# Spectral mixing and a maxout layer in one kernel: all stores on one queue, in more and smaller blocks

## The chip, the cores and the metric

The kernel runs on one core of one Trainium2 chip. The metric is device time in microseconds (us) from launch to end. Three runs of the kernel before took 436.36, 440.05 and 441.28 us, a median of 440.05 us. One more execution was profiled; all durations below come from that one.

A core has five engines that run their own instruction streams: TensorE (PE, matmuls; PEld is its weight load), VectorE (DVE), ScalarE (ACT), GpSimd (POOL) and SyncE (SP), which only starts transfers. SP and ACT start transfers on hardware queues, POOL on a software queue. 16 DMA engines move the data.

## What is computed

```python
def _attn_ref(x):                       # x: 8 x 3072 x 256
    X = np.fft.fft(x, axis=1)
    X = np.fft.fft(X, axis=2)
    return X.real.astype(np.float32)

def _moe_ref(x, w1, w2, w3, w_out):     # 24576 x 256, w: 256 x 768, w_out: 768 x 256
    h = np.maximum(np.maximum(x @ w1, x @ w2), x @ w3)
    return (h @ w_out).astype(np.float32)

def reference(**kwargs):
    ...
    x = attn_out.reshape(B * S, D)
    return _moe_ref(x=x, **moe_kwargs)
```

Each of 8 batches has 3072 tokens of 256 values. A two-dimensional Fourier transform is taken and its real part goes through three linear maps, a maximum over them, and an output map.

## The kernel before

**Mixing.** The transform over the sequence is split in two factors, and the transform over the 256 features is folded into the weights (`g_all`, `gd_all`, `gw`). For batch b the class `Mix` has these steps. `s` multiplies the loaded `xt` by a small table (through PSUM into `tb`). `y` writes `tb` to a DRAM buffer `db`, and `z` reads it back transposed into `yb` (four transfers, two for each value of `hh`); both are issued by SP, and z waits until y has landed. `x0` fills one column of `yb`. `k` makes the token tables `tE` (even part) and `tO` (odd part) from `yb`, in three column groups; after each odd group SP writes one row of `tO` to DRAM (`vd`), and `v` broadcasts it from there over 128 partitions (`vb`).

**Symmetry.** Token n and token 3072 - n have the same even part and opposite odd parts. So one pass over 1536 columns gives both: rows "plus" (n) and "minus" (the mirror rows).

**Units.** The main loop has 18 units per batch: 3 blocks of 512 columns by 6 chunks of 128 hidden values, 144 units in all. `begin` multiplies for the plus rows and writes `hp`; `finish` adds the difference `gd_all` x `tO` onto the same PSUM tiles (L489) and writes `hm`. In a plain unit this takes six matmuls of 512 columns, two ScalarE activations and two VectorE maxima. In a split unit (`is_split`) the third product is made ahead by `third` (L824), two units early: two matmuls, one ScalarE copy (`odd`), one VectorE sum with `vb` (`even`, L833), and two GpSimd sums `plus` and `minus` (L837). Then `begin` needs two matmuls, `finish` one, and each a VectorE operation (L846, L858). Odd units from 7 on are split, and even units 0, 4 and 8 of each batch but the first. `prev` holds the unit whose `finish` is still to come. If it is split, `finish` comes before the next `begin`; otherwise after it.

**Output.** When a block's six units are done, its output matmuls (`l2_block`, L553 and L576) are put in a queue and ten are taken in each following unit (`l2_some`). So a block's results are complete at the end of the sixth unit after it: block 2 of the batch before in unit 5, block 0 in unit 11, block 1 in unit 17. They stand in one of three buffers (`obufs`: `obuf` and the two halves of `kq`) as 128 partitions by 8 slots of 256 values: slots 0 to 3 plus rows, 4 to 7 minus rows.

**Order of the rows.** The columns of the tables, and so the partitions of the output buffers, are numbered by `ramp`. A slot has 96 partitions of one residue modulo 32 and 32 partitions of another. Each group is cut into two halves in opposite order, so that both the plus rows (ascending) and the minus rows (descending within each half) can be described by a regular pattern.

**Stores before.** `stores_plus` gives four transfers per block (48, 16, 48 and 16 partitions), for block 2 six, with one of 47 and one of 48 single rows. SP issues them as soon as the block is complete. `stores_minus` gives two per block (three for block 2), each over both halves in one pattern (`back`, with a leading count of 2). They are put in `waiting`, and GpSimd issues them in the next unit (`scatter`).

**What else is on the queues.** GpSimd issues the x loads (L115), in units 9 or 10 and 11 of a batch and 0 and 1 of the next. SP issues y (units 2 and 3), z0 and z1 (units 6 and 7), `vd` and `v` (units 12 to 16), each at its place in the program, and SP works strictly in this order.

**The last block.** `l2_last` takes the sub-blocks in the order 1, 2, 3, 0. Minus rows are computed there in flipped order (`flipped`, from reversed copies of `tE` and `tO`, and `hm` written reversed), and its stores go to ACT, SP and POOL in turn: twelve after sub-block 3 and eight at the end.

The table `ahead` (L802) says in which unit a mixing step for the next batch is emitted.

Of the kernel before, what the change touches and what calls it, by code (L numbers as in the profile page):

```python
# [20 lines left out]
def _reduce(nc, w, v, q, period):  # L21

    nc.vector.tensor_scalar(out=q, in0=v, scalar1=1.0 / period, scalar2=ROUND,
                            op0=ALU.mult, op1=ALU.add)
    nc.vector.tensor_scalar(out=q, in0=q, scalar1=-ROUND, scalar2=-period,
                            op0=ALU.add, op1=ALU.mult)
    nc.vector.tensor_tensor(out=w, in0=v, in1=q, op=ALU.add)


def _parts(g):  # L30
# [10 lines left out]
def kernel(  # L41
# [9 lines left out]
    nc = tc.nc  # L51

    B, S, D = x.shape
# [83 lines left out]
    def iota(t, pattern, base=0, cm=0):  # L137
        nc.gpsimd.iota(t, pattern, base=base, channel_multiplier=cm,
                       allow_small_or_imprecise_dtypes=True)
# [17 lines left out]
    def ramp(g):  # L157
        kv = kvec[:, 512 * g:512 * g + 512].rearrange("p (s c) -> p s c", s=4)
        n = 4 if g < 2 else 3
        iota(kv[:, 0:n, 0:96].rearrange("p s (a j) -> p s a j", a=2),  # L160
             [[1, n], [-1536, 2], [32, 48]], base=4 * g + 1 + 1536)
        iota(kv[:, :, 96:128].rearrange("p s (a j) -> p s a j", a=2),
             [[1, 4], [-512, 2], [32, 16]], base=12 + 1024 * g + 512)
        if g == 2:
            iota(kv[:, 3, 0:96].rearrange("p (a j) -> p a j", a=2), [[-768, 2], [16, 48]],
                 base=784)
            iota(kvec[:, NHALF:NHALF + 1], [[0, 1]], base=0)

    dvec = gen.tile([128, 128], FP32, tag="dvec")
# [339 lines left out]
    def rows_of(b):  # L509

        mine = out[b * S:(b + 1) * S, :]
        return mine, mine.rearrange("(j r) d -> j r d", r=32)

    def back(v):
        return v.rearrange("(a j) r d -> a j r d", a=2)[:, ::-1]

    def stores_plus(b, blk, buf, s0=0, s1=4):

        mine, v = rows_of(b)
        n = s1 if blk < 2 else min(s1, 3)  # L520
        for a in range(2):
            j = 48 - 48 * a
            yield v[j:j + 48, 4 * blk + 1 + s0:4 * blk + 1 + n, :], buf[48 * a:48 * a + 48, s0:n, :]
            j = 32 * blk + 16 - 16 * a
            yield v[j:j + 16, 12 + s0:12 + s1, :], buf[96 + 16 * a:112 + 16 * a, s0:s1, :]
        if n < s1:
            yield mine[784:784 + 46 * 16 + 1:16, :], buf[0:47, 3, :]
            yield mine[16:16 + 47 * 16 + 1:16, :], buf[48:96, 3, :]

    def stores_minus(b, blk, buf):  # L530

        mine, v = rows_of(b)
        n = 4 if blk < 2 else 3
        r = 32 - 4 * blk
        yield back(v[0:96, r - n:r, :]), buf[0:96, 8 - n:8, :]
        yield back(v[64 - 32 * blk:96 - 32 * blk, 17:21, :]), buf[96:128, 4:8, :]
        if n < 4:
            yield back(mine[NHALF:S - 15:16, :].unsqueeze(1)), buf[0:96, 4:5, :]

    def stores_turned(b, buf, s0, s1):  # L540

        mine, v = rows_of(b)
        n = min(s1, 3)
        for a in range(2):
            j = 48 - 48 * a
            yield v[j:j + 48, 24 - n:24 - s0, :], buf[80 - j:128 - j, 8 - n:8 - s0, :]
            yield v[16 - 16 * a:32 - 16 * a, 21 - s1:21 - s0, :], buf[16 * a:16 * a + 16, 8 - s1:8 - s0, :]
            if n < s1:
                yield mine[S - 768 - 768 * a:S - 15 - 768 * a:16, :], buf[80 - j:128 - j, 4, :]

    def l2_hidden(po, hcols):
        for jc in range(NJC):
# [4 lines left out]
    def l2_block(b, blk, hp, hm, te, to):  # L557

        buf = obufs.pop(0)
        obufs.append(buf)  # L560
        for sub in range(4):
            slot = blk * 4 + sub
            cp = slice(slot * 128, slot * 128 + 128)
            sp = slice(sub * 128, sub * 128 + 128)
            if sub % 2 == 0:
                pl = ps_f.tile([128, 512], FP32, name="pl", tag="ps")
                for i in range(2):
                    ci = (slot + i) * 128
                    nc.tensor.matmul(pl[:, i * 256:(i + 1) * 256], te[:, ci:ci + 128],
                                     gw[:, 0:256], start=True, stop=True)  # L570
                    yield
                even = even_pool.tile([128, 512], FP32, name="even", tag="even")
                nc.scalar.copy(out=even, in_=pl)
            lin = even[:, (sub % 2) * 256:(sub % 2 + 1) * 256]
            po = ps_o.tile([128, 512], FP32, name="po", tag="po")
            nc.tensor.matmul(po, to[:, cp], gw[:, 256:768], start=True, stop=True)  # L576
            yield
            yield
            yield from l2_hidden(po[:, 0:256], lambda jc: hp[:, jc, sp])
            yield from l2_hidden(po[:, 256:512], lambda jc: hm[:, jc, sp])  # L580
            nc.vector.tensor_tensor(  # L581
                out=buf[:, sub:8 - sub:7 - 2 * sub, :], in0=po.rearrange("p (h c) -> p h c", h=2),
                in1=lin.unsqueeze(1).to_broadcast([128, 2, 256]), op=ALU.add)
        for (dst, src) in stores_plus(b, blk, buf):
            store(nc.sync, dst, src)
        waiting.extend(stores_minus(b, blk, buf))

    def l2_last(hp, hm, te, to, flipped):

        buf = obufs.pop(0)  # L590
        ter, tor = flipped
        for sub in (1, 2, 3, 0):
            slot = 8 + sub
            cp = slice(slot * 128, slot * 128 + 128)
            sp = slice(sub * 128, sub * 128 + 128)
            sm = slice((3 - sub) * 128, (4 - sub) * 128)
            for (h, tev, tov, wo, hid) in (
                    (0, te[:, cp], to[:, cp], gw[:, 256:512], lambda jc: hp[:, jc, sp]),
                    (1, ter[:, sm], tor[:, sm], gw[:, 512:768], lambda jc: hm[:, jc, sm])):
                if h == 0 or sub == 0:  # L600
                    po = ps_o.tile([128, 512], FP32, name="po", tag="po")
                ph = po[:, h * 256:(h + 1) * 256]
                nc.tensor.matmul(ph, tev, gw[:, 0:256], start=True, stop=False)
                yield
                nc.tensor.matmul(ph, tov, wo, start=False, stop=True)
                yield
                yield from l2_hidden(ph, hid)
                stores = []
                if sub == 0:
                    nc.vector.tensor_copy(out=buf[:, 7 * h, :], in_=ph)  # L610
                    stores = (stores_turned(B - 1, buf, 0, 1) if h else
                              stores_plus(B - 1, 2, buf, 0, 1))
                elif h:
                    nc.vector.tensor_copy(out=buf[:, sub:8 - sub:7 - 2 * sub, :],  # L614
                                          in_=po.rearrange("p (h c) -> p h c", h=2))
                    if sub == 3:
                        stores = [*stores_plus(B - 1, 2, buf, 1, 4),
                                  *stores_turned(B - 1, buf, 1, 4)]
                for k, (dst, src) in enumerate(stores):
                    store((nc.scalar, nc.sync, nc.gpsimd)[k % 3], dst, src)  # L620

    def l2_mid():

# [23 lines left out]
        store(nc.sync, out[0: S * (B - 1) + 1: S, :], ot[0:B, 0:256])  # L647

    l2_queue = []
    waiting = []  # L650

    def scatter():

        while waiting:
            store(nc.gpsimd, *waiting.pop(0))

    def l2_some(n):
        while n > 0 and l2_queue:
            try:
# [131 lines left out]
    for b in range(2, B):  # L791
# [3 lines left out]
        for ch in range(8):  # L795
# [4 lines left out]
              7: ("z0", "z1"), 12: ("x",), 13: ("kO0",), 14: ("v0", "kE0", "kO1"),  # L800
              15: ("v1", "kE1"), 16: ("kO2",), 17: ("v2", "kE2", "end")}
    ahead = {1: ("s0", "s1"), 2: ("s2", "y0", "s3", "s6"), 3: ("s4", "s5", "y1", "u"),  # L802
             6: ("z0",), 7: ("z1",), 11: ("x",), 12: ("kO0",), 13: ("v0", "kE0", "kO1"),
             14: ("v1", "kE1"), 15: ("kO2",), 16: ("v2", "kE2", "end")}
    for b in range(B - 1):
        for u, whats in (ahead0, ahead)[min(b, 1)].items():
# [4 lines left out]

    def is_split(g):
        if g % 2 == 0:
            return UNITS <= g < B * UNITS and g % UNITS in (0, 4, 8)
        return 7 <= g < B * UNITS

    def operands(g):
# [46 lines left out]
    for g in range(B * UNITS):  # L864
# [4 lines left out]
        if jc == 0:  # L869
            hp = h_pool.tile([128, NJC, TOKB], BF16, name="hp", tag="hp")  # L870
            hm = h_pool.tile([128, NJC, TOKB], BF16, name="hm", tag="hm")
            if last:
                flipped = []
                for t, name in ((mm.tE, "tEr"), (mm.tO, "tOr")):
                    fl = h_pool.tile([128, TOKB], BF16, name=name, tag=name)
                    flipped.append(fl)
                    nc.gpsimd.tensor_copy(fl, t[:, 3 * TOKB - 1: 2 * TOKB - 1: -1])
        if prev is not None and is_split(prev[0]):
            finish(*prev)
            prev = None  # L880
        pses = begin(g, hp[:, jc, :])
        if prev is not None:
            finish(*prev)
        prev = (g, pses, hm[:, jc, ::-1] if last else hm[:, jc, :])
        for lead in (1, 2):
            if is_split(g + lead) and (lead == 1) == (g + lead == 7):
                third(g + lead)
        scatter()
        l2_some(10)
        if b == B - 1 and u in (1, 3):  # L890
            if u == 1:
# [8 lines left out]
            l2_queue.append(l2_last(hp, hm, mm.tE, mm.tO, flipped) if last else  # L900
                            l2_block(b, blk, hp, hm, mm.tE, mm.tO))

    scatter()
    l2_some(1000)

# [28 lines left out]
```

## Time and profile before

| | |
|---|---|
| median of three runs | 440.05 us |
| the profiled execution's own time | 433.8 us |
| its span, first to last instruction | 432.0 us |
| mean granted TensorE clock | 0.975 |
| PE busy | 383.7 us, 89% of the span |
| VectorE / GpSimd / ScalarE busy | 330.4 / 308.2 / 248.6 us |
| hardware queue q1 (SP) | 26.58 MB, 23.6% of 16 engines' span |
| software queue q0 (POOL) | 26.67 MB, 34.8% of 16 engines' span |
| store issues on POOL | 59, of them 43 from `kq` with 28.4 us busy |
| POOL stores, issue to landing | 8.1 to 15.8 us, median 11.7 |

The busy share in 40 slices shows when an engine works; PEclk is the granted TensorE clock in tenths.

```profile
PE   7799997998979979999979969999499999999990
PEclk9999999999999989999999989999799999999996
DMA  8999563867538582687747582575413644322343
```

The chain of work that ended last, by engine, shows 57% PE and 21% DMA:

```profile
PE 57%; DMA 21%; DVE 8%; issue 4%; ACT 3%; POOL 2%; SPq 2%; DVEq 0%; POOLq 0%; ACTq 0%
```

How to read the rest: in lists of waits, "A <- B: 13.5, 4, 5.5" says that A's engine stood idle for 13.5 us in 4 cases, 5.5 at most, until B had ended. In timelines the first number is the start from the span's begin, the second the duration in us; "SPq" is SP's own stream, and a DMA line there is the issue, not the transfer. TensorE matmuls are pipelined, and the profile's PE durations overlap: 512 columns take 0.22 us one behind the other.

### The profile page before, as it was taken

What the parts mean: (1) busy time and instruction counts of PE and PEld (TensorE: products, weight loads), DVE (VectorE), ACT (ScalarE), POOL (GpSimd) and SP (SyncE); (2) the same over time, 40 slices, a digit from 0 to 9 for tenths busy, and PEclk for the clock granted to TensorE, in tenths of its full rate; (3) what the DMA queues carried; (4) which work ended last, traced back from release to release, by engine and by line L of the source; (5) the groups of instructions that cost most, each with busy time, mean ns of one, the idle gap of its engine ahead of it and who ended that gap; (6) DMA issues with size and microseconds to landing.
All of it is one profiled execution on the core that took longest, in us unless ns stands there. A gap on an engine that the chain in (4) does not pass through costs nothing.

```text
span 432.0 us, 8171 instructions
## 1 busy us (share of the span) xinstructions
PE 383.7 (89%) x2769; PEld 238.6 (55%) x2818; DVE 330.4 (76%) x551; ACT 248.6 (58%) x454; POOL 308.2 (71%) x336
## 2 busy tenths in 40 slices
PE   7799997998979979999979969999499999999990
PEld 2455664565645546565645636565265666665670
DVE  7887976886688857798778847789277997898860
ACT  6887794666736756575836746576365537433400
POOL 9981676987487946988677955977358776879741
PEclk9999999999999989999999989999799999999996
DMA  8999563867538582687747582575413644322343
GB/s 126 162 179 182 132 138 92 137 145 171 123 82 164 158 170 71 121 168 161 147 96 152 140 180 86 104 143 133 130 46 83 147 122 113 86 66 60 89 110 106
DMA packets 72244, 54.24 MB, mean 126 GB/s; under 512 B 46717, under 2 KB 64900, under 8 KB 71347
## 3 DMA queue, kind: packets, MB, share of 16 engines
q0 software_dynamic: 39680, 26.67, 34.8%
q1 hardware_dynamic: 32106, 26.58, 23.6%
q10 hardware_dynamic: 416, 0.48, 0.4%
q8 instruction: 22, 0.36, 0.3%
q14 instruction: 20, 0.16, 0.1%
HBM read 36.95 MB, written 30.81 MB: 157 GB/s over the span
## 4 chain that ended last, share of the span: by engine, by line
PE 57%; DMA 21%; DVE 8%; issue 4%; ACT 3%; POOL 2%; SPq 2%; DVEq 0%; POOLq 0%; ACTq 0%
PE po L553 19%; DMA yb<-db 12%; PE pse L489 9%; DMA vb<-vd 4%; PE e L828 4%; PE pse L482 4%; PE d L830 3%; PE pse L483 3%; DMA vd<-tO 3%; PE pse L844 3%; PE po L576 3%; PE pse L845 3%; PE ps L393 2%; DVE hp L846 2%; DVE hm L858 2%
## 5 line engine op out<-in xcount | busy, mean ns | idle before, releaser
L837 POOL TENSOR_TENSOR plus<-even,odd 128x512 bf16<-128x512 f32 x90 | 114.4, 1271 | 105.6 <-DVE even L833 96.1
L837 POOL TENSOR_TENSOR minus<-even,odd 128x512 bf16<-128x512 f32 x90 | 114.1, 1268 | 0.0
L832 ACT ACTIVATE odd<-d 128x512 f32<-128x512 f32 x90 | 53.8, 598 | 66.7 <-PE d L830 57.7
L553 PE MATMUL po<-wout_bf,hp 128*128 128x256 bf16 x576 | 86.3, 273 | 0.0
L846 DVE SCALAR_TENSOR_TENSOR hp<-pse,plus 128x512 bf16<-128x512 f32 x90 | 61.7, 686 | 24.5 <-PE pse L845 11.4
L553 PE MATMUL po<-wout_bf,hm 128*128 128x256 bf16 x576 | 80.3, 277 | 0.0
L495 ACT ACTIVATE stmp<-pse 128x512 bf16<-128x512 f32 x108 | 64.6, 601 | 26.4 <-PE pse L483 11.3
L489 PE MATMUL pse<-tO,gd_all 128*128 128x512 bf16 x197 | 67.9, 387 | 11.1 <-DVE hp L846 9.1
L833 DVE SCALAR_TENSOR_TENSOR even<-vb,wcol,e 128x512 f32<-128x512 bf16 x90 | 66.4, 738 | 7.9 <-DMA vb<-vd 7.9
L553 PEld LDWEIGHTS <-hp 128*128 128x128 bf16 x576 | 56.5, 98 | 26.4 <-issue 0.3
L858 DVE SCALAR_TENSOR_TENSOR hm<-pse,minus 128x512 bf16<-128x512 f32 x90 | 61.7, 685 | 11.8 <-PE pse L489 10.2
L553 PEld LDWEIGHTS <-hm 128*128 128x128 bf16 x576 | 57.2, 99 | 18.2 <-issue 2.1
L496 DVE TENSOR_TENSOR hp<-pse,stmp 128x512 bf16<-128x512 f32 x54 | 37.2, 689 | 26.7 <-ACT stmp L495 22.5
L496 DVE TENSOR_TENSOR hm<-pse,stmp 128x512 bf16<-128x512 f32 x54 | 37.2, 690 | 10.2 <-ACT stmp L495 8.1
L581 DVE TENSOR_TENSOR kq<-po,even 128x512 f32<-128x512 f32 x60 | 41.0, 684 | 0.1
L122 ACT COPY xt<-xt 64x762 bf16<-64x762 bf16 (+1 forms) x48 | 39.7, 838 | 1.0
L483 PE MATMUL pse<-tO,g_all 128*128 128x512 bf16 x101 | 38.3, 379 | 0.5 <-issue 0.2
L482 PE MATMUL pse<-tE,g_all 128*128 128x512 bf16 x100 | 37.9, 379 | 0.7 <-DVE tE L460 0.4
L828 PE MATMUL e<-tE,g_all 128*128 128x512 bf16 x89 | 34.5, 387 | 3.2 <-DVE even L833 2.9
L576 PE MATMUL po<-gw,tO 128*128 128x512 bf16 x92 | 35.1, 382 | 0.0
L830 PE MATMUL d<-tO,gd_all 128*128 128x512 bf16 x90 | 34.9, 387 | 0.2
L499 POOL DMA_DIRECT2D out_dram<-kq x43 | 28.4, 666 | 5.8 <-DVE kq L614 3.6
(167 smaller groups left out, 500.4 us busy)
## 6 DMA issues: line engine op xcount, KB each, us to landing
xt<-in_x_dram POOLq DMA_DIRECT2D x14, 384.0 KB, 9.7
db<-tb SPq DMA_DIRECT2D x21, 192.0 KB
out_dram<-obuf SPq DMA_DIRECT2D x16, 192.0 KB
out_dram<-obuf POOLq DMA_DIRECT2D x8, 384.0 KB, 12.8
out_dram<-kq SPq DMA_DIRECT2D x16, 192.0 KB
out_dram<-kq POOLq DMA_DIRECT2D x8, 384.0 KB, 11.1
vb<-vd SPq DMA_DIRECT2D x23, 128.0 KB
xt<-in_x_dram POOLq DMA_DIRECT2D x7, 400.0 KB, 8.4
```

The source lines that it names most:

```text
L482: nc.tensor.matmul(pse[:, 0:n], g_all[:, jc, 2 * i, :], te, start=True, stop=False)
L483: nc.tensor.matmul(pse[:, 0:n], g_all[:, jc, 2 * i + 1, :], to, start=False, stop=True)
L489: nc.tensor.matmul(pse, gd_all[:, jc, i, :], to, start=False, stop=True, skip_group_check=True)
L495: nc.scalar.activation(out=stmp[:, 0:n], in_=pses[0][:, 0:n], func=AX.Relu)
L496: nc.vector.tensor_tensor(out=dst, in0=src3, in1=stmp[:, 0:n], op=ALU.max)
L553: nc.tensor.matmul(po, hcols(jc), wout_bf[:, jc * 256:(jc + 1) * 256], start=False, stop=(jc == NJC - 1), skip_group_check=True)
L828: nc.tensor.matmul(e3, g_all[:, jc, 2, :], te, start=True, stop=True)
L832: nc.scalar.activation(out=odd3, in_=d3, func=AX.Copy, scale=-0.5)
L833: nc.vector.scalar_tensor_tensor(out=even3, in0=vb, scalar=wcol[:, jc:jc + 1], in1=e3, op0=ALU.mult, op1=ALU.add)
L837: nc.gpsimd.tensor_tensor(out=dst, in0=even3, in1=odd3, op=op)
L846: nc.vector.scalar_tensor_tensor(out=dst, in0=pse2, scalar=0.0, in1=sums[g][0], op0=ALU.max, op1=ALU.max)
L858: nc.vector.scalar_tensor_tensor(out=dst, in0=pses[0], scalar=0.0, in1=sums.pop(g)[1], op0=ALU.max, op1=ALU.max)
```

## The change

- The order of rows is cut differently: the 96 partitions into 6 blocks of 16 (`MAIN`), the 32 into 4 blocks of 8 (`LOW`), and the extra slot of block 2 into 5 blocks of 19 and one single row (`LATE`). `ramp` and all store patterns follow.
- `stores_plus` gives one transfer per block of rows: 10 per block of columns, and 16 for block 2. `stores_minus` still gives one per group, over all its blocks at once (leading count 6, 4 or 5).
- SP issues plus and minus rows one after the other when the block is complete; `waiting` and `scatter` go.
- In the last block the plus rows are now the flipped ones (`hp` written reversed, `stores_turned` over plus slots), the minus rows are natural, and its 7 + 4 stores go to ACT and SP in turn.
- z0 and z1 of the next batch are emitted in unit 5, ahead of that unit's stores in SP's order.
- Unit 10 of each batch but the first is split as well.
- If both the waiting unit and the new one are split, `begin` of the new one now comes before `finish` of the waiting one.

```diff
+MAIN = (6, 16)
+LOW = (4, 8)
+LATE = (5, 19)
...
-    def back(v):
-        return v.rearrange("(a j) r d -> a j r d", a=2)[:, ::-1]
-
-    def stores_plus(b, blk, buf, s0=0, s1=4):
+    def back(v, n):
+        return v.rearrange("(a j) r d -> a j r d", a=n)[:, ::-1]
+
+    def stores_plus(b, blk, buf):
+
+        mine, v = rows_of(b)
+        n = 4 if blk < 2 else 3
+        for at, j0, (na, nj), r, m in ((0, 0, MAIN, 4 * blk + 1, n), (96, 32 * blk, LOW, 12, 4)):
+            for a in range(na):
+                j = j0 + nj * (na - 1 - a)
+                yield v[j:j + nj, r:r + m, :], buf[at + a * nj:at + a * nj + nj, 0:m, :]
+        if n < 4:
+            for a in range(5):
+                m = 1 + 19 * (4 - a)
+                yield mine[16 * m:16 * (m + 18) + 1:16, :], buf[19 * a:19 * a + 19, 3, :]
+            yield mine[NHALF:NHALF + 1, :], buf[95:96, 3, :]
+
+    def stores_minus(b, blk, buf, s0=0, s1=4):
...
+        r = 32 - 4 * blk
+        yield back(v[0:96, r - n:r - s0, :], MAIN[0]), buf[0:96, 8 - n:8 - s0, :]
+        yield (back(v[64 - 32 * blk:96 - 32 * blk, 21 - s1:21 - s0, :], LOW[0]),
+               buf[96:128, 8 - s1:8 - s0, :])
         if n < s1:
...
+            yield (back(mine[NHALF + 16:S - 15:16, :].unsqueeze(1), LATE[0]), buf[0:95, 4:5, :])
...
         for (dst, src) in stores_plus(b, blk, buf):
             store(nc.sync, dst, src)
-        waiting.extend(stores_minus(b, blk, buf))
+        for (dst, src) in stores_minus(b, blk, buf):
+            store(nc.sync, dst, src)
...
-                    store((nc.scalar, nc.sync, nc.gpsimd)[k % 3], dst, src)
+                    store((nc.scalar, nc.sync)[k % 2], dst, src)
...
-             6: ("z0",), 7: ("z1",), 11: ("x",), 12: ("kO0",), 13: ("v0", "kE0", "kO1"),
+             5: ("z0", "z1"), 11: ("x",), 12: ("kO0",), 13: ("v0", "kE0", "kO1"),
...
-            return UNITS <= g < B * UNITS and g % UNITS in (0, 4, 8)
+            return UNITS <= g < B * UNITS and g % UNITS in (0, 4, 8, 10)
...
-        if prev is not None and is_split(prev[0]):
+        if prev is not None and is_split(prev[0]) and not is_split(g):
             finish(*prev)
             prev = None
-        pses = begin(g, hp[:, jc, :])
+        pses = begin(g, hp[:, jc, ::-1] if last else hp[:, jc, :])
         if prev is not None:
             finish(*prev)
-        prev = (g, pses, hm[:, jc, ::-1] if last else hm[:, jc, :])
+        prev = (g, pses, hm[:, jc, :])
...
-        scatter()
```

More of the change, by code (lines that the diff above doesn't have):

```diff
@@ L159, in ramp @@
         n = 4 if g < 2 else 3
[L160 to L163, printed above, removed]
+        (a, j), (la, lj), (ea, ej) = MAIN, LOW, LATE
+        iota(kv[:, 0:n, 0:96].rearrange("p s (a j) -> p s a j", a=a),
+             [[1, n], [-32 * j, a], [32, j]], base=4 * g + 1 + 32 * (96 - j))
+        iota(kv[:, :, 96:128].rearrange("p s (a j) -> p s a j", a=la),
+             [[1, 4], [-32 * lj, la], [32, lj]], base=12 + 1024 * g + 32 * (32 - lj))
         if g == 2:
-            iota(kv[:, 3, 0:96].rearrange("p (a j) -> p a j", a=2), [[-768, 2], [16, 48]],
-                 base=784)
+            iota(kv[:, 3, 0:95].rearrange("p (a j) -> p a j", a=ea), [[-16 * ej, ea], [16, ej]],
+                 base=16 * (96 - ej))
+            iota(kv[:, 3, 95:96], [[0, 1]], base=NHALF)
             iota(kvec[:, NHALF:NHALF + 1], [[0, 1]], base=0)
@@ L512, in rows_of @@
         return mine, mine.rearrange("(j r) d -> j r d", r=32)
-    def back(v):
-        return v.rearrange("(a j) r d -> a j r d", a=2)[:, ::-1]
-    def stores_plus(b, blk, buf, s0=0, s1=4):
+    def back(v, n):
[13 more added lines that the diff above has]
+    def stores_minus(b, blk, buf, s0=0, s1=4):
         mine, v = rows_of(b)
         n = s1 if blk < 2 else min(s1, 3)
[L521 to L525, printed above, removed]
-        if n < s1:
[L527 to L538, printed above, removed]
+        r = 32 - 4 * blk
+        yield back(v[0:96, r - n:r - s0, :], MAIN[0]), buf[0:96, 8 - n:8 - s0, :]
+        yield (back(v[64 - 32 * blk:96 - 32 * blk, 21 - s1:21 - s0, :], LOW[0]),
+               buf[96:128, 8 - s1:8 - s0, :])
+        if n < s1:
+            yield (back(mine[NHALF + 16:S - 15:16, :].unsqueeze(1), LATE[0]), buf[0:95, 4:5, :])
     def stores_turned(b, buf, s0, s1):
@@ L543, in stores_turned @@
         n = min(s1, 3)
[L544 to L549, printed above, removed]
+        yield back(v[0:96, 9 + s0:9 + n, :], MAIN[0]), buf[32:128, s0:n, :]
+        yield back(v[64:96, 12 + s0:12 + s1, :], LOW[0]), buf[0:32, s0:s1, :]
+        if n < s1:
+            yield back(mine[16:NHALF - 15:16, :].unsqueeze(1), LATE[0]), buf[33:128, 3:4, :]
+            yield mine[NHALF:NHALF + 1, :], buf[32:33, 3, :]
     def l2_hidden(po, hcols):
@@ L597, in l2_last @@
             for (h, tev, tov, wo, hid) in (
-                    (0, te[:, cp], to[:, cp], gw[:, 256:512], lambda jc: hp[:, jc, sp]),
-                    (1, ter[:, sm], tor[:, sm], gw[:, 512:768], lambda jc: hm[:, jc, sm])):
+                    (0, ter[:, sm], tor[:, sm], gw[:, 256:512], lambda jc: hp[:, jc, sm]),
+                    (1, te[:, cp], to[:, cp], gw[:, 512:768], lambda jc: hm[:, jc, sp])):
                 if h == 0 or sub == 0:
@@ L610, in l2_last @@
                     nc.vector.tensor_copy(out=buf[:, 7 * h, :], in_=ph)
-                    stores = (stores_turned(B - 1, buf, 0, 1) if h else
-                              stores_plus(B - 1, 2, buf, 0, 1))
+                    stores = (stores_minus(B - 1, 2, buf, 0, 1) if h else
+                              stores_turned(B - 1, buf, 0, 1))
                 elif h:
@@ L616, in l2_last @@
                     if sub == 3:
-                        stores = [*stores_plus(B - 1, 2, buf, 1, 4),
-                                  *stores_turned(B - 1, buf, 1, 4)]
+                        stores = [*stores_turned(B - 1, buf, 1, 4),
+                                  *stores_minus(B - 1, 2, buf, 1, 4)]
                 for k, (dst, src) in enumerate(stores):
-                    store((nc.scalar, nc.sync, nc.gpsimd)[k % 3], dst, src)
+                    store((nc.scalar, nc.sync)[k % 2], dst, src)
     def l2_mid():
@@ L649 @@
     l2_queue = []
[L650 to L655, printed above, removed]
     def l2_some(n):
@@ L901 @@
                             l2_block(b, blk, hp, hm, mm.tE, mm.tO))
-    scatter()
     l2_some(1000)
```

## The prediction

> **What bounds the kernel now.** I read the page's chain of waits first, then the waits of the engines, then a table with one stretch for each batch, then SyncE's own timeline. Everything is made against the profiled execution: its span is 432.0 us, its own time 433.8 us, so 1.8 us lie around the span; the median of the three runs, 440.05 us, is 6.25 us above it. I work out a difference on the profile and add it to the median.
>
> The waits name two transfers:
>
> ```profile
> PE ps L458 <- ACT yb L448: 13.5, 4, 5.5
> PE pse L489 <- DVE hp L846: 9.1, 15, 1.2
> PE e L828 <- DVE even L833: 2.9, 2, 1.5
> ...
> ACT yb L447 <- DMA yb<-db: 20.7, 5, 7.0
> ...
> DVE even L833 <- DMA vb<-vd: 7.9, 3, 3.0
> ```
>
> Columns: total us, times, longest. TensorE waits for ScalarE's `yb`, and ScalarE waits for the gather `yb<-db` (the z step). Second comes the `vb` broadcast, without which VectorE cannot start the third sums of the next batch.
>
> The stretches run from the first `hp` write of a batch to that of the next, batches 1 to 6:
>
> ```profile
> 73.61:123.73 50.12, 44.81 (x325) 27.95 (x331) 38.40 (x61) 30.71 (x55) 37.30 (x38) 1.00 0.64 136
> 123.73:174.09 50.36, 45.51 (x324) 28.34 (x330) 38.79 (x62) 30.65 (x55) 37.38 (x38) 0.97 0.63 135
> 174.09:222.28 48.19, 44.99 (x329) 28.12 (x333) 38.46 (x62) 30.80 (x56) 37.28 (x38) 1.00 0.66 141
> 222.28:273.32 51.04, 45.59 (x324) 28.30 (x330) 38.70 (x61) 30.72 (x55) 37.38 (x38) 0.97 0.60 133
> 273.32:327.15 53.83, 46.65 (x328) 28.86 (x332) 38.88 (x62) 30.82 (x56) 36.17 (x36) 0.94 0.48 112
> 327.15:372.61 45.46, 44.26 (x328) 27.98 (x332) 38.58 (x61) 24.20 (x47) 34.89 (x34) 1.00 0.46 114
> ```
>
> After each stretch stand its length, then PE, PEld, DVE, ACT and POOL busy, then the granted clock. Batch 6 has neither wait: 45.46 us with TensorE busy for 44.26. That is the floor. The five before it lie 4.66, 4.90, 2.73, 5.58 and 8.37 above it, together 26.2 us. Part of this is clock: it is 0.51 for 3.5 us right after the PE waits of 2.9 and 3.5 us, and for 6.9 us after the one of 5.5.
>
> SyncE in batch 1:
>
> ```profile
> 85.78 3.11 SPq L415 DMA_DIRECT2D db<-tb  x1
> 88.99 4.87 SPq L499 DMA_DIRECT2D out_dram<-kq  x6
> 93.95 4.42 SPq L421 DMA_DIRECT2D yb<-db  x4
> 102.85 3.51 SPq L499 DMA_DIRECT2D out_dram<-obuf  x4
> 108.31 0.23 SPq L463 DMA_DIRECT2D vd<-tO  x1
> 113.28 0.34 SPq L467 DMA_DIRECT2D vb<-vd  x1
> ```
>
> The gather stands behind six stores and the first `vd` behind four. `vd` takes 4.97 us until the broadcast that waits for it can go; where nothing is under way (batch 5, 311.94 to 313.19) it takes 1.25.
>
> **The gather ahead of the stores (z at unit 5).** z waits for the y write `db<-tb`, whose last packet ends 18.8 to 19.9 us after the batch's first `hp` in batches 1 to 5 and 15.4 after it in batch 6, which has no x loads. By the trace's packet records z0 already issues 0.6 to 1.5 us after that, so the move itself gains at most 1.5 us, plus up to 2.4 for z1 (its wait for unit 7). More comes from what is no longer in front or beside: the 47-row store ahead of z runs on one DMA engine, row after row 41 ns apart until 97.91, and one of the gather's five trains of 7,680 B packets starts at 97.92, right behind it. The POOL mirror stores, of whose packets at most 5 or 6 run at once for two stores, hold their few engines for some 9 us (76.5 to 85.7). Without these I take y at +17 (between 15.4 and 19.9) and the gather's own 4.3 us on its busiest engine (5 x (0.291 + 0.328) + 2 x 0.62): `yb` at about +23.5, where x0 wants it at +28.2 (batch 6). So the `yb` wait goes; bounds 20 to 26 us of the 26.2.
>
> **Mirror stores off POOL.** 59 issues leave POOL, 43 from `kq` (28.4 us) and 16 from `obuf` (0.67 us each), 39 us; unit 10 brings 7 x (1.271 + 1.268) = 17.8 back. POOL is covered either way: VectorE waits only 2.3 us in all for `plus`. Nothing on the path.
>
> **Unit 10 split.** Five 512-column matmuls in place of six: 7 x 0.22 = 1.5 us off TensorE, which is the floor. VectorE gets 7 x (738 + 686 + 685 - 2 x 689) ns = 5.1 us more, 0.7 per batch beside 38.6 busy of 45.5; if that cover were gone it would cost those 5. I take -1.5.
>
> **Products ahead of the last difference.** It can end at most the 9.1 us that L489 waits for `hp`; batch 6 has 0.8 of them. The ring of two `pse2` buffers bounds it the other way at about as much. I take -1.
>
> **SyncE's queue and the engine that all short stores share.** A block now issues 10 + 2 stores (block 2: 16 + 3) on SP in place of 4 (6), at some 0.45 us each (four from 326.66 to 328.53): 12 take 5.4 us, and the first `vd` of the batch is queued behind the twelve of block 0. These are ready at +29.1 (batch 6: 356.22), `tO` at +31.3; so `vd` leaves at +34.5 at the earliest. Nor is SP free to run: the hardware queues use eight semaphores in turn, so each transfer waits until the eighth before it has landed (SP waits 6.5 us for this already).
>
> How many engines carry a store follows from its leading count: the 47-row store runs on 1, the 25-partition gather on 5, POOL's two-block stores on about 2. So the six blocks of a mirror store run on between 2 and 16 engines; I take 6, for the four-block ones 4, and for the 19-row ones 1, like the 47-row one, because that count is what sets all known ones. The gather's fifth train shows that the one-engine store and the five-engine one share an engine. I call it the first engine, and `vd`, one row, is on it too. The Trainium skill's page DMA: Bandwidth & Descriptors (Why a DMA increments its semaphore by 16 and not by 1) gives the same as a rule, the largest count up to 16 that divides both sides, on the lowest-numbered engines, and so 6, 4 and 1; the trace agrees for 5 and 1.
>
> On that engine, by packet (4,096 B 159 ns, 3,072 B 121, 1,024 B 41.5): block 2 takes 6 x 0.121 + 4 x 0.159 + 95 x 0.0415 for plus rows and 16 x 0.121 + 8 x 0.159 + 19 x 0.0415 for mirror rows, 9.3 us; block 0 takes (10 + 16 + 8) x 0.159 = 5.4. With the gather's 4.3 that is 19 us between z and `vd`, and 24 in batches 1 to 4, where two x loads (2 x 1.02, 48 x 0.060) fall into it. Starting at +18.1 (y and 1.1 to the first packet), with some 2 us in which SP waits for landings, `vd` lands near +45. `vb` lands after between 1.6 us (1.25 as above and eight packets of 46 ns) and 6.3 (as in three batches now); I take 2.3, since the POOL stores beside it are gone: +47.3. Batch 6 uses it at +40.7 (367.80). VectorE then waits 6.5 us in batches 1 to 4, by the same sum without the loads 4.3 in batch 5, and 2.8 in batch 6 with its earlier y. Bounds: with no gaps 4.3, 0.3 and 0.3; with 6 us for `vb`, as now, about 10, 8 and 6. I put the wait on the batch as it is: what TensorE has in hand beside it and what a half clock behind it adds (1.7 us for 3.5) are taken to cancel.
>
> **The end.** The last VectorE copy ends at 421.4, the last packet at 429.1. The first engine then gets block 1's 5.4, the last block's 2 x (1.94 + 0.97 + 0.79) and 2 x (0.66 + 0.33): 14.8 us, and SP hands it block 1's mirror rows only 4 us after 414.4. It ends near 431.7 to 432.7; fewer issues (11 for 20) may give some back. Bounds 0 to +4; I take +2.6.
>
> **The sum.** Batches 1 to 4: 4 x (45.5 + 6.5) - 199.7 = +8.3; batch 5: 49.8 - 53.8 = -4.0; batch 6 +2.8; end +2.6; unit 10 and order -2.5. Together +7, so 447 us: the `vb` wait takes the place of the `yb` wait.
>
> **The rivals.**
> 1. Faster: the first engine is not the bottleneck, because mirror stores spread over more engines than I take or because `vd` slips through between the loads' packets. It decides from the point where `vb` lands by +40.7, that is `vd` by +38.4. For it: packets of two queues alternate, and the broadcast itself loses the POOL stores beside it (its 6 us end with them). Then 26 of waits go, the 2.5 too, the end costs 2.6: 414 us at full effect; with 1 to 3 us of wait left per batch 420 to 432; I take 424. In this sense the Trainium skill's same page (Issuing engines are not separate DMA queues) says that which engine issues saves sequencer time alone; by that rule moving the stores costs only the 5.4 us of issue, and the time would be 424. The trace is against it as far as order within one queue goes (the train behind the 47 rows). 0.35.
> 2. No change: 5 us of wait in batches 1 to 4 and 3 in batch 5, 440 us. 0.13.
> 3. The change does not do what it says: y still lands at +19.5, since it and not the queue holds z; then `yb` is just in time and `vb` later by 2 us more, 455 us. It is part of the slower side: 0.10 of its 0.52.
>
> **Numbers.** Forecast (slower, vb wait) 0.42, rival 3 0.10, rival 2 0.13, rival 1 0.35. About 1% is what a measurement of this kernel can tell. Faster 0.35, within 1% 0.13, slower 0.52. The forecast's own range is 441 to 456; reaching down into rival 1 until 2 in 10 are left out, 423 to 456.
>
> **What would show it.** Right: `ACT yb <- DMA yb` near zero; `DVE even <- DMA vb` at 25 to 40 us over six or seven times; `vd` issued on SP later than +38; half-clock stretches after unit 17 instead of unit 12. Wrong: `vb` waits under 10 us in all, and batches at 46 to 47 us; or a `yb` wait that stays; or POOL `plus` holding `hp` in units 7 to 11.

## The result, and the profile after

The changed kernel takes 502.03 us (median of four runs, 497.44 to 504.00) against 440.09 us before. The ratio is 1.155, with a 95% interval of 1.138 to 1.172. So it is slower, by about 62 us. The profiled execution took 502.85 us, its span is 501.1 us, 69.1 us over the span before. Where several executions of one kernel are given, the ratio leaves out those more than 1.5% above its fastest, and the median keeps them.

The stretches from one batch's first `hp` write to the next one's, batches 1 to 6 (columns as before: length, PE, PEld, DVE, ACT and POOL busy, granted clock, DMA share, GB/s):

```profile
75.40:133.45 58.05, 45.02 (x327) 27.81 (x327) 38.91 (x62) 30.33 (x54) 35.06 (x33) 0.91 0.55 117
133.45:195.27 61.82, 46.90 (x332) 28.60 (x331) 38.91 (x62) 30.32 (x54) 35.07 (x33) 0.89 0.53 109
195.27:256.27 61.00, 46.72 (x332) 28.53 (x331) 38.92 (x62) 30.33 (x54) 35.08 (x33) 0.89 0.54 111
256.27:317.12 60.85, 46.95 (x332) 28.58 (x331) 38.91 (x63) 30.33 (x54) 35.10 (x33) 0.89 0.55 112
317.12:374.38 57.26, 47.23 (x332) 28.73 (x331) 39.01 (x63) 30.33 (x54) 33.88 (x31) 0.92 0.48 105
374.38:425.70 51.32, 45.98 (x332) 28.39 (x331) 39.01 (x63) 23.63 (x45) 32.62 (x29) 0.97 0.43 101
```

They are 7.9, 11.5, 12.8, 9.8, 3.4 and 5.9 us longer than before, 51.3 together. Everything up to batch 1 adds 1.8 us, batch 7 adds 0.7. From the last `hp` to the end it is 35.1 us instead of 19.8, another 15.3. The sum is 69.1. The waits of the compute engines show what fills the batches:

```profile
POOL plus L839 <- DVE even L835: 156.3, 52, 15.9
ACT odd L834 <- PE d L832: 80.0, 55, 4.2
DVE even L835 <- DMA vb<-vd: 79.2, 7, 15.6
...
PE pse L496 <- DVE hp L848: 66.3, 7, 13.8
```

The wait for the gather (`ACT yb <- DMA yb`, 20.7 us before) is gone. The wait for the `vb` broadcast has grown from 7.9 to 79.2 us in seven cases, one for each batch that has a next one. TensorE's 66.3 us in seven cases are the same stalls seen from behind: it waits for `hp`, which stands behind `even` on VectorE. Take the `vb` waits of batches 1 to 6 (12.7, 15.6, 14.9, 14.6, 10.7 and 6.2 us) off the stretches, and 45.1 to 46.6 us are left, the floor of before.

SyncE's timeline in batch 2 (first `hp` at 133.45) shows why `vb` is late:

```profile
142.25 10.47 SPq L422 DMA_DIRECT2D db<-tb  x4
154.77 1.43 SPq L428 DMA_DIRECT2D yb<-db  x4
156.25 15.05 SPq L506 DMA_DIRECT2D out_dram<-kq  x19
171.39 11.27 SPq L506 DMA_DIRECT2D out_dram<-obuf  x12
182.76 0.83 SPq L470 DMA_DIRECT2D vd<-tO  x1
188.50 0.37 SPq L474 DMA_DIRECT2D vb<-vd  x1
```

`tO` is ready at 166.97, but `vd` is issued at 182.76, behind 31 stores that take 26.4 us to pass. It then needs 5.7 us to land. What SyncE itself waits for:

```profile
SPq L474 <- DMA vd<-tO: 58.4, 23, 4.8
SPq L506 <- DMA out_dram<-kq: 44.2, 31, 18.1
...
SPq L506 <- DMA yb<-db: 21.1, 23, 2.1
```

Before the change, stores waited 6.5 us for earlier stores. Now they wait 44.2 us for stores (18.1 of them in one wait at the end) and 21.1 us for the gather. The stalls of batches 1 to 6 also lower the granted clock (0.89 to 0.97 in the table). These are stretches inside batch 2 (same columns; the first is the stall, the second what follows it):

```profile
182.70:191.50 8.80, 0.00 (x0) 0.00 (x0) 0.00 (x0) 0.00 (x0) 0.00 (x0) 0.60 0.25 72
...
191.50:195.00 3.50, 1.45 (x6) 0.71 (x6) 3.44 (x6) 0.40 (x1) 2.55 (x3) 0.50 0.19 58
```

During the stall the DMA engines are busy for a quarter only, so it is not total bandwidth that is short.

### The profile page after: what moved, and what is told of

The parts are those of the page before. It is cut to its first block, busy times and chain, and to the rows that moved or that the text cites. A ratio compares the mean times of both kernels' runs of the same rounds, so it can differ in the third digit from the quotient of the medians.

```text
span 501.1 us, 8366 instructions
## 1 busy us (share of the span) xinstructions
PE 391.7 (78%) x2811; PEld 239.9 (48%) x2811; DVE 333.5 (67%) x558; ACT 245.5 (49%) x447; POOL 287.1 (57%) x292
## 4 chain that ended last, share of the span: by engine, by line
PE 39%; DMA 30%; DVE 11%; SPq 7%; issue 3%; POOL 2%; ACT 1%; DVEq 0%; POOLq 0%; ACTq 0%
PE po L561 12%; DMA out_dram<-kq 8%; DMA vd<-tO 8%; SPq L506 7%; DMA yb<-db 6%; PE pse L496 5%; DMA vb<-vd 4%; PE pse L846 4%; DMA xt<-in_x_dram 3%; DVE hp L848 3%; DVE hm L860 3%; PE e L830 3%; PE d L832 3%; PE pse L847 3%; PE pse L489 2%
## 5 line engine op out<-in xcount | busy, mean ns | idle before, releaser
L839 POOL TENSOR_TENSOR plus<-even,odd 128x512 bf16<-128x512 f32 x97 | 123.2, 1270 | 175.3 <-DVE even L835 156.3
L835 DVE SCALAR_TENSOR_TENSOR even<-vb,wcol,e 128x512 f32<-128x512 bf16 x97 | 71.6, 738 | 79.2 <-DMA vb<-vd 79.2
L839 POOL TENSOR_TENSOR minus<-even,odd 128x512 bf16<-128x512 f32 x97 | 123.1, 1269 | 0.0
L496 PE MATMUL pse<-tO,gd_all 128*128 128x512 bf16 x191 | 67.0, 391 | 66.3 <-DVE hp L848 66.3
L848 DVE SCALAR_TENSOR_TENSOR hp<-pse,plus 128x512 bf16<-128x512 f32 x97 | 66.8, 688 | 37.1 <-PE pse L847 29.4
L860 DVE SCALAR_TENSOR_TENSOR hm<-pse,minus 128x512 bf16<-128x512 f32 x97 | 66.0, 681 | 2.2 <-PE pse L496 1.5
L502 ACT ACTIVATE stmp<-pse 128x512 bf16<-128x512 f32 x94 | 56.1, 600 | 20.4 <-PE pse L490 10.8
L581 ACT COPY even<-pl 128x512 f32<-128x512 f32 x46 | 26.8, 582 | 78.8 <-PE pl L577 78.4
L577 PEld LDWEIGHTS <-tE 128*128 128x128 bf16 x92 | 9.3, 102 | 79.2 <-issue 69.9
L503 DVE TENSOR_TENSOR hp<-pse,stmp 128x512 bf16<-128x512 f32 x47 | 32.3, 686 | 7.7 <-ACT stmp L502 3.0
L503 DVE TENSOR_TENSOR hm<-pse,stmp 128x512 bf16<-128x512 f32 x47 | 32.4, 689 | 6.1 <-ACT stmp L502 4.6
```

What stands on the lines that cost most here:

```text
L496: nc.tensor.matmul(pse, gd_all[:, jc, i, :], to, start=False, stop=True, skip_group_check=True)
L502: nc.scalar.activation(out=stmp[:, 0:n], in_=pses[0][:, 0:n], func=AX.Relu)
L503: nc.vector.tensor_tensor(out=dst, in0=src3, in1=stmp[:, 0:n], op=ALU.max)
L835: nc.vector.scalar_tensor_tensor(out=even3, in0=vb, scalar=wcol[:, jc:jc + 1], in1=e3, op0=ALU.mult, op1=ALU.add)
L839: nc.gpsimd.tensor_tensor(out=dst, in0=even3, in1=odd3, op=op)
L848: nc.vector.scalar_tensor_tensor(out=dst, in0=pse2, scalar=0.0, in1=sums[g][0], op0=ALU.max, op1=ALU.max)
```

## The experiments

Two theories say why `vd` and `vb` are late. A: too many issues on SyncE, in an order that puts `vd` last. B: the mirror stores run on few DMA engines, always the same, and those are overloaded. Theory C concerns the end: a semaphore that ScalarE's and SyncE's stores share. Experiments 1 to 5 are single executions, the others medians of four. In 3 and 4 some rows land in other places of the output than the reference has them. Each result stands beside a run of the kernel before on the same chip: 440.86 us in the first four, 436.28 (median of seven) in the next four, 437.60 (of seven) in the last three.

**1. `vd` and `vb` on GpSimd**

```diff
-                nc.sync.dma_start(out=vds[self.b % 2][:, cs], in_=self.tO[0:1, cs])
+                nc.gpsimd.dma_start(out=vds[self.b % 2][:, cs], in_=self.tO[0:1, cs])
...
-            nc.sync.dma_start(out=self.vb[:, cs],
+            nc.gpsimd.dma_start(out=self.vb[:, cs],
```

> The changed kernel with the vd write and the vb broadcast issued by GpSimd instead of SyncE; all stores stay on SyncE. Theory A (SyncE's order: the first vd is late because it is queued behind 31 stores): the vb waits of VectorE fall from 79 us to under 15 and the time from 502 to 435-450 us. Theory B (the first few DMA engines, which carry every mirror store, are too busy, whichever queue a transfer comes from): vd and vb still pass those engines behind the stores; the vb waits stay above 40 us and the time above 465.

Measured: 483.7 us, `vb` waits 31.7 us in seven cases. The waits lie between the two theories (under 15, above 40), the time is in B's range. GpSimd's timeline in batch 1 shows why this separates less than it was meant to (in brackets the idle time before an instruction and what ended it):

```profile
115.29 0.74 POOL L120 DMA_DIRECT2D xt<-in_x_dram  x1
116.20 0.51 POOL L470 DMA_DIRECT2D vd<-tO  x1 [0.17 <-issue]
...
128.18 0.58 POOL L474 DMA_DIRECT2D vb<-vd  x1 [7.74 <-DMA vd<-tO]
128.75 0.50 POOL L470 DMA_DIRECT2D vd<-tO  x1
136.47 0.59 POOL L474 DMA_DIRECT2D vb<-vd  x1 [7.22 <-DMA vd<-tO]
```

No store is ahead of `vd` in GpSimd's queue, but other transfers are. By the semaphore records the x load issued just before the first `vd` lands at 127.52 and `vd` at 127.89; the broadcast ahead of the second `vd` lands at 135.84 and `vd` at 136.18. So these waits of more than 7 us can be order in GpSimd's own queue or a busy engine, and the run does not tell which. GpSimd, blocked meanwhile, makes `plus` late (VectorE waits 29.6 us for it), so the kernel gains only 18 us.

**2. Block 0's stores behind the first `vb`**

```diff
-        for (dst, src) in stores_plus(b, blk, buf):
-            store(nc.sync, dst, src)
-        for (dst, src) in stores_minus(b, blk, buf):
-            store(nc.sync, dst, src)
+        held.extend([*stores_plus(b, blk, buf), *stores_minus(b, blk, buf)])
+        if blk or b == B - 1:
+            release()
...
             mm.v(int(what[1]))
+            if what == "v0":
+                release()
```

> The changed kernel with the twelve stores of block 0 issued on SyncE after the first vb broadcast instead of before it. Theory A: vd leaves SyncE some 11 us earlier (the twelve took 171.4 to 182.7 in batch 2), the vb waits fall to 10-25 us and the time to 440-455. Theory B: the ring of the first engine still holds block 2's mirror rows; 4 us of each wait go at most, 45-55 us of vb waits stay, 470-480 us.

Measured: 467.37 us, `vb` waits 24.5 us. The waits fall as A said (10 to 25); the time does not reach A's 440 to 455, because the `yb` wait comes back (13.5 us in five batches) and the end stays long (36.6 us). The order on SyncE is thus part of the cause, but the stores only move their delay to the next transfer.

**3. The same stores, mirror rows on 16 engines**

```diff
-        yield back(v[0:96, r - n:r - s0, :], MAIN[0]), buf[0:96, 8 - n:8 - s0, :]
-        yield (back(v[64 - 32 * blk:96 - 32 * blk, 21 - s1:21 - s0, :], LOW[0]),
+        yield v[0:96, r - n:r - s0, :], buf[0:96, 8 - n:8 - s0, :]
+        yield (v[64 - 32 * blk:96 - 32 * blk, 21 - s1:21 - s0, :],
                buf[96:128, 8 - s1:8 - s0, :])
```

> The changed kernel with the mirror rows of the 96- and the 32-partition group written in ascending order, so that one regular pattern covers the group (these rows land in other places of the output; bytes and number of transfers are the same) and, by the count rule, all 16 engines carry it instead of 6 and 4. Theory A (number and order of issues on SyncE): nothing changes, vb waits 60-80 us, time 490-505. Theory B (load of the first engines: block 2 and block 0 together 7.0 us less on the busiest): vb waits fall below 35 us and the time to 445-465.

Measured: 422.75 us; B's direction, and more than it asked for. What changed can be counted: each transfer on the hardware queue leaves one 4-byte packet per engine. The changed kernel has 4,353 of them, which is exactly the sum with 6, 4 and 5 engines for mirror stores, 1 for 19 rows, 16 and 8 for plus stores. This kernel has 4,883, that is 23 x 10 + 25 x 12 more (23 stores go from 6 to 16 engines, 25 from 4 to 16). All larger packets are the same in number and size. The order in which the mirror rows are written changes with the pattern, and that was not tried apart from the spread. Its waits:

```profile
DVE even L835 <- DMA vb<-vd: 11.6, 4, 4.6
```

and SyncE in batch 2 (first `hp` at 119.55):

```profile
136.79 12.03 SPq L506 DMA_DIRECT2D out_dram<-kq  x19
149.58 8.01 SPq L506 DMA_DIRECT2D out_dram<-obuf  x12
158.85 0.23 SPq L470 DMA_DIRECT2D vd<-tO  x1
160.08 0.35 SPq L474 DMA_DIRECT2D vb<-vd  x1
```

The same 31 stores now take 20.8 us from the first to the last (for 1.3 of them SyncE waits for VectorE's results), and `vd` lands in 1.2 us instead of 5.7.

**4. Plus rows in one transfer per group**

```diff
-            for a in range(na):
-                j = j0 + nj * (na - 1 - a)
-                yield v[j:j + nj, r:r + m, :], buf[at + a * nj:at + a * nj + nj, 0:m, :]
+            yield back(v[j0:j0 + na * nj, r:r + m, :], na), buf[at:at + na * nj, 0:m, :]
...
-            for a in range(5):
-                m = 1 + 19 * (4 - a)
-                yield mine[16 * m:16 * (m + 18) + 1:16, :], buf[19 * a:19 * a + 19, 3, :]
+            yield back(mine[16:NHALF - 15:16, :].unsqueeze(1), LATE[0]), buf[0:95, 3:4, :]
```

> The changed kernel with the plus rows of a group also written by one transfer over all blocks (the pattern of the mirror rows; these rows land in other places of the output): 4 issues per block instead of 12, 7 instead of 19 for block 2, but the plus rows too on 6, 4 and 5 engines. Theory A: 11 + 8 fewer issues ahead of vd; vb waits fall below 30 us, time 440-460. Theory B: the busiest engine has 1.3 us less at block 2 and 2.2 us more at block 0; vb waits stay at 75-90 us, time 495-510.

Measured: 460.6 us, `vb` waits 47.8 us in seven cases. Between the two, on time just above A's range (440 to 460): fewer issues take away 31 us of `vb` waits, although the plus rows now run on few engines too. SyncE's waits for `vd` to land rise from 58.4 to 95.5 us, 14.1 at most, as one expects if the row is behind more stores on its engine. I put the `vb` waits that are left down to that load.

**5. The last block's stores all on SyncE**

```diff
-                    store((nc.scalar, nc.sync)[k % 2], dst, src)
+                    store(nc.sync, dst, src)
```

> The changed kernel with the eleven stores of the last block all on SyncE instead of alternating with ScalarE. The changed kernel has 35.1 us from the last hp to the end (19.8 before), with an 18 us wait of SyncE at block 0's eleventh store, which has the semaphore that a later store of ScalarE sets. Theory C (a semaphore shared by the two hardware queues holds SyncE until ScalarE's stores of the last block have landed): that wait goes, the end takes 20-26 us, the time falls to 486-493. Rival (the end is long because all mirror rows of the last blocks go to the same few engines): the end stays at 31-36 us, the time at 497-504.

Measured: 497.33 us; the end takes 26.3 us instead of 35.1, just above C's bound (26) and below the rival's (31). The time is 4 us over what C gave and just inside the rival's range, because all that stands ahead of the last `hp` was 3.3 us longer in this execution. The end of the changed kernel, SyncE:

```profile
455.10 24.60 SPq L506 DMA_DIRECT2D out_dram<-obuf  x12
480.31 14.93 SPq L506 DMA_DIRECT2D out_dram<-kq  x17
```

and with all stores on SyncE:

```profile
458.40 5.70 SPq L506 DMA_DIRECT2D out_dram<-obuf  x12
471.44 18.70 SPq L506 DMA_DIRECT2D out_dram<-kq  x23
```

Block 0's twelve stores take 24.6 us in the first and 5.7 in the second; the wait of 18.1 us is gone. In the first, the eleventh of them has semaphore 115, which ScalarE's store at 473.61 sets; SyncE goes on at 478.25. So without this wait the end is 9 us shorter. But it is not the wait alone. With the mirror rows spread (experiment 3) SyncE shows the same wait of 18.1 us, and the end takes 24.2 us:

```profile
385.90 24.01 SPq L506 DMA_DIRECT2D out_dram<-obuf  x12
410.00 8.06 SPq L506 DMA_DIRECT2D out_dram<-kq  x17
```

There the 17 stores behind the wait pass in 8.1 us instead of 14.9. So the 15 us of the longer end come from the wait and from the slow stores behind it together; taking away either gives back 9 to 11 us.

**6. Mirror rows back on GpSimd, in the new blocks**

```diff
-        for (dst, src) in stores_minus(b, blk, buf):
-            store(nc.sync, dst, src)
+        waiting.extend(stores_minus(b, blk, buf))
```

(with `scatter` as before)

> The changed kernel with the mirror rows issued by GpSimd in the next unit, as before the change, but in the new six and four blocks. Theory B (SyncE's ring and its low-numbered engines are overloaded by the mirror rows): vb waits fall from 79 us to 10-30, and with the 18 us wait at the end perhaps still there the time is 425-445. Theory A (number of issues on SyncE, 10 and 16 instead of 12 and 19): vb waits 60-75, time 485-500.

Measured: 430.79 us (428.24 to 433.83), ratio to before 0.986 (0.976 to 0.995); `vb` waits 14.3 us, both as B said. That is no clear change against the kernel before. So two or three stores per block on another queue are worth some 71 us; in batches 1 to 6 `vd` now lands 1.2 to 2.0 us after its issue. The trace does not tell on which engines the stores from GpSimd's queue run, so this run does not separate the load of the engines from the order on SyncE's queue; experiment 3 does.

Taken together, against the 502 us of the changed kernel: the spread of the mirror rows is worth 79 us (3), fewer issues 41 us even with more stores on few engines (4), and the order of block 0's stores 35 us (2). Both theories hold in part, and the gains do not add up.

**7. Parts of the change on the kernel before**

Gather first:

```diff
-             6: ("z0",), 7: ("z1",), 11: ("x",), 12: ("kO0",), 13: ("v0", "kE0", "kO1"),
+             5: ("z0", "z1"), 11: ("x",), 12: ("kO0",), 13: ("v0", "kE0", "kO1"),
```

> The kernel before with one part of the change, z0 and z1 emitted in unit 5, ahead of block 2's stores on SyncE. My reading of the trace before: the 47-row store no longer delays one train of the gather by 2.5 us and z1 no longer waits for unit 7: the yb waits fall from 20.7 us to 5-10, the vb waits rise a little, time 424-434 (ratio 0.965-0.985). Rival (y's landing alone sets the gather): yb waits stay at 15-20 us, time within 1% of 440.

Measured: 423.35 us, ratio 0.969 (0.960 to 0.977). So this part alone makes the kernel faster, by about 3%, with the ratio as forecast. In its profiled execution (428.81 us) ScalarE waits 3.2 us for the gather, less than the 5 to 10 of the forecast, and the `vb` waits rise from 7.9 to 16.9 us, so a part of the gain is lost there.

All three parts that are not about stores:

> The kernel before with three parts of the change: gather first, unit 10 split, and products ahead of the last difference for two split units in a row; stores as before. If the last two are worth the 2.5 us that I took: 2 to 3 us under the kernel with the gather first alone, 421-432. Rival: unit 10's two extra sums on GpSimd, which still issues the mirror stores, and 0.7 us more VectorE per batch hold hp: 3 to 6 us above it.

Measured: 431.38 us, ratio 0.989 (0.982 to 0.995), 8 us above the gather alone: the rival's direction, and more than its 3 to 6. To see which of the two it is, each was run without the other.

> The kernel before with the gather first and with products ahead of the last difference for two split units in a row, without unit 10. The three parts together took 431.4 us, the gather alone 423.4: 8 us are lost by order and unit 10. Theory D (the order costs: VectorE's hm comes one operation later and begin of the next unit waits for its PSUM tile): 428-432, and TensorE's wait for hm at the first product of a split unit at 10 us or more. Rival (unit 10 costs): 421-425.

> The kernel before with the gather first and unit 10 split, in the old order. Theory D: 420-424, since a split unit has one matmul less. Rival (unit 10 costs, by GpSimd's sums that come too late or VectorE's 0.7 us per batch): 427-432.

Measured: 424.78 us (ratio 0.971, 0.963 to 0.978) and 424.43 us (0.971, 0.962 to 0.979). Neither costs or gains anything clear of the gather alone; only both together do. So theory D is wrong on the time, though the wait that it named is there. TensorE's waits with the order alone:

```profile
PE pse L844 <- DVE hm L858: 14.6, 14, 1.6
PE pse L489 <- DVE hp L846: 3.1, 5, 1.5
```

and with both:

```profile
PE pse L844 <- DVE hm L858: 17.6, 26, 1.6
PE pse L489 <- DVE hp L846: 8.8, 5, 2.7
```

In the new order, with or without unit 10, TensorE waits for the tile that `hm` frees, where it waited for `hp` in the old order (19.5 us in 23 cases with unit 10 alone). With unit 10 the units 7 to 11 are five split ones in a row, and these waits come in 26 cases instead of 14. But they grow by 3.0 us only. The waits for `hp` grow by 5.7 us, and VectorE's `vb` waits are 12.4 us with both, 7.2 with the order alone and 17.8 with unit 10 alone. So these waits of TensorE are 8.7 us more than with the order alone, and most of that is not `hm`. Why both together cost 8 us stays open.

**8. A version that beats both**

The kernel before, with the gather first, and block 0's stores held until the first `vb` is issued:

```diff
-        for (dst, src) in stores_plus(b, blk, buf):
-            store(nc.sync, dst, src)
-        waiting.extend(stores_minus(b, blk, buf))
+        held.append((b, blk, buf))
+        if blk or b == B - 1:
+            release()
...
             mm.v(int(what[1]))
+            if what == "v0":
+                release()
```

> The kernel before with the gather first, and the stores of block 0 (on both queues) issued only after the first vb broadcast. If the vb wait that is left in the kernel with the gather alone (16.9 us in five cases) comes from these stores ahead of and beside vd: vb waits under 7 us, time 413-419 (ratio to before 0.945-0.965). Rival (it comes from the x loads in the same stretch): vb waits 12-17, time 421-426.

Measured: 412.09 us (410.12 to 413.35), ratio to before 0.942 (0.934 to 0.949). That is a little better than forecast. No `vb` wait is left in its trace, so the rival, the x loads, is out: they stand in the program as before. TensorE still waits 4.3 us for `yb`. SyncE in batch 2 (first `hp` at 118.60):

```profile
140.17 6.50 SPq L499 DMA_DIRECT2D out_dram<-kq  x6
151.61 0.23 SPq L463 DMA_DIRECT2D vd<-tO  x1
156.10 0.35 SPq L467 DMA_DIRECT2D vb<-vd  x1
156.54 4.74 SPq L499 DMA_DIRECT2D out_dram<-obuf  x4
```

Now `vd` and `vb` stand ahead of block 0's stores, and the page of this execution (span 410.8 us) shows a granted clock of 0.9 or more until the last slice:

```profile
PEclk9999999999999999999999999999999999999996
```

## Why the prediction was right in kind and wrong in size

- **The `yb` wait goes: right.** It is gone, and what the batches need without the `vb` wait (45.1 to 46.6 us) is near the floor that I took (45.5). The gather alone on the old kernel shows the gain. But I took the y write to land at +17; the gather, which waits for it, issues at +17.8 in batch 1 and at +20.9 to +21.4 in batches 2 to 5. With the mirror rows spread (experiment 3) it is +15.7 to +17.0. So the mirror rows on few engines hold up y too. A late y was rival 3's condition; it came true, and by another cause than rival 3 had.
- **The `vb` wait takes its place: right in kind, the size was the error.** The term was 6.5 us in batches 1 to 4, 4.3 in batch 5 and 2.8 in batch 6; measured are 12.7 to 15.6, 10.7 and 6.2, 42 us too few in these six. The step that failed is "with some 2 us in which SP waits for landings". From the gather's first packet until `vd` has landed, the sum has 24 us of packets and these 2, so 26 (19 and 2 in batches 5 and 6). By the trace's packet records and SyncE's timeline 32.0 to 32.9 us pass in batches 1 to 4, and 28.6 in batches 5 and 6. SyncE's own waits for landings between the gather and `vd` are, in batch 2:

```profile
SPq L506 <- DMA out_dram<-kq: 4.5, 5, 1.7
SPq L506 <- DMA yb<-db: 3.9, 4, 1.9
```

These are 8.4 us; in batch 1 they are 11.0. If the 24 us are right, the 2 us were 8 to 9 there (and 9.6 in batches 5 and 6). A later start adds to that: the first packet is at +22.2 in batch 2, where I had +18.1. So `vd` lands at +55.0 instead of +45. That the 24 us of packets are right by themselves is not shown, since the trace does not name the engines. My reading is that I added up the first engine's packets as if it were kept fed: a store is issued only when the eighth before it has landed, that landing can stand behind other stores on the same engine, and so engine and queue wait for each other in turn. No run tries this part alone.

- **Engines per store: right.** 6, 4, 5 and 1 give the packet count exactly. That the few-engine transfers share engines is what experiments 3 and 4 need. The Trainium skill's page DMA: Bandwidth & Descriptors (Why a DMA increments its semaphore by 16 and not by 1) has the rule; the counts here agree, and no count tells which engines they are.
- **Rival 1's price: right, its condition not met.** With mirror rows on more engines I gave 424 us; experiment 3 took 422.75. That the two meet within 2 us is partly luck: it is one execution, and its end is 4.4 us longer than before where I took 2.6. By the rule of the Trainium skill (DMA: Bandwidth & Descriptors, Issuing engines are not separate DMA queues) that another issuing engine saves sequencer time alone, the change would have taken 424; 502 against 430.79 with mirror rows on GpSimd shows that here the issuing queue decided much more.
- **The end: wrong.** +2.6 was taken, +15.3 measured. I had the eight semaphores in the working, but not that a store of ScalarE can hold one that SyncE needs next. That wait and the slow stores behind it make the end long together (experiments 3 and 5).
- **Unit 10 and order: wrong.** -2.5 was taken; on the old kernel each alone changes nothing and both together cost 8 us. I had costed each by itself. In the changed kernel neither was taken out.
- **Mirror stores off POOL: right** that GpSimd's freed time buys nothing; experiment 6 puts them back, and it is far faster.
- **The clock: about right.** I let it cancel against overlap. The half clock is long (0.50 from 184.4 to 198.1 around the stall of batch 2), but the stretches of batches 1 to 6 without their `vb` waits come to 2.8 us over six floors in all.

## What to carry to other kernels

Before moving transfers onto one queue, write down for each the number of engines it runs on and add up the busiest engine between two transfers that a compute engine waits for; then count the queue's own waits for earlier landings as well; in batch 2 here they were 8.4 us and came nearly on top of an estimated 24. Put the small transfer on which the next stage hangs ahead of the bulk stores, in program order: together with the gather first, that was worth 5.8% here. Parts of a bundle should be timed one by one, since one good part was hidden under the bad one, and also in pairs, since two that cost nothing alone cost 8 us together.

## What was not expected of the hardware

- One row of 1 KB (`vd` in batch 2) needed 5.7 us to land while the DMA engines were busy for a quarter only, and 1.2 us when the same mirror rows ran on 16 engines.
- Two hardware queues can hold each other up through a shared semaphore: SyncE stood for 18.1 us until a store of ScalarE had landed that was issued only 13.5 us into the wait.
